# Chunked attention and a gated feed-forward network on one core: sums of the weights formed by GpSimd during the first pair, seven products one step earlier

## The chip, the core and the metric

The kernel runs on one core of a Trainium2 chip. The core has five engines that run side by side and wait for one another by semaphores: TensorE (PE, matrix products into PSUM), VectorE (DVE), ScalarE (ACT), GpSimd (POOL) and SyncE (SP, which here only issues DMAs). The metric is the device time of one execution in microseconds, lower is better; several executions are timed and the median is given.

## What is computed

Attention within chunks of 64 rows, for 8 batches, 8 heads, 576 rows and 64 columns a head; its output, heads side by side, is a matrix of 4608 rows and 512 columns, and goes through a gated network of width 1536:

```python
scores = scale * np.matmul(q_c, k_c.transpose(0, 1, 2, 4, 3))
attn = np.exp(scores - np.max(scores, axis=-1, keepdims=True))
attn = attn / (np.sum(attn, axis=-1, keepdims=True) + 1e-09)
out = np.matmul(attn, v_c)
...
g = x @ w_gate
silu = g * (1.0 / (1.0 + np.exp(-g)))
return (silu * (x @ w_val) @ w_out).astype(np.float32)
```

## The kernel before

**Rows and steps.** The 4608 rows are nine groups of 512 ("batches" a0, a1 and so on in the code; `N` is 512). The width of 1536 is cut into twelve *steps* of 128 (`NF` is 12). In a step f, the gate and the value of 128 columns are formed for a group (512 columns of moving data), multiplied after the Silu, and projected back to 512 columns, added up over the steps in PSUM. Every operand is a pair of a high and a low part, and every product takes three matmuls (low by high, high by low, high by high).

**Seven products instead of eight.** Two groups together can be treated as a 2 x 2 block product, by Winograd's form of Strassen's method: 7 products of half the depth instead of 8. It needs sums and differences of the blocks of x (`x1`, `x2`, `x4`, `x5` beside the plain blocks) and of the four quarters of a step's weights (`Quarters.sums`: three instructions, then a high part by a cast, `upper`, and a low part by a subtraction, `lower`). In matmuls of 512 columns a step of two groups has 48 products plainly and 42 with seven; the projection of one group adds 12.

**The stages.**
1. *Opening*, groups 0 and 1: their attention, then the steps 0 to 11 while the weights arrive in raw form and are split (`Up`, `Out`). Steps below `SEVEN` (6) are plain (the loop `for f in range(1, SEVEN)`, products at L494), the later ones use seven products (`first_seven`, products at L898). Only group 0 is projected here (L572 to L574); group 1's products are put off to DRAM. During steps 2 to 5, DVE and ACT form the sums of x (class `Raw`; L812, L815, L821, L825), and in every step those of the next step's weights (L157 to L159, L171, L174), which are saved to DRAM for the pairs (`kept_t`), as are the weights themselves (`save_w`, `kept_w`).
2. *Projection of group 1*, with the attention of group 2 beside it.
3. *The single batch*, group 2: twelve plain steps in the order 4 to 11, 0 to 3, the attention of groups 3 and 4 beside it. GpSimd forms sums of the output weights (class `WeightSums`, L1385 to L1394) and, at the fifth and sixth place, the weight sums of step 0 (`FirstQuarters`, L193).
4. *Three pairs*, groups 3 and 4, 5 and 6, 7 and 8: seven products a step (`both_steps`, `gated_pair`), with the left half of the projection; then the right half, itself by Strassen's method (`second_steps`, 30 *units* of a kind and a couple of steps, L560). Each step loads its weights and weight sums from DRAM (`load_weights`), two steps ahead, when the buffers are free. The attention of the next pair is spread over the places of the current one: dictionaries `middle`, `beside`, `behind` and `bursts` say what is added at which step, and where in it.

**Order of the work.** PE, ACT and DVE run their instructions in the order of the program text. SP does so in the opening alone; afterwards SP's and GpSimd's instructions are placed by a planner at the time at which it expects them ready, so a load may be issued long before its place in the text. All queues are in order once placed: an instruction that waits holds all those behind it.

**Buffers.** Tiles with the same tag share memory, and a tile waits for the release of its predecessor. The tags of the change: `w0` to `w11` (weights of the steps, reused; `moved(i)` is `w` of (i + 4) mod 12, so `moved(11)` is `w3`), `w8`, `w9`, `th`, `turned`, and the banks `ps_a`, `ps_gv`, `ps_o`. In `gated_pair`, ACT copies the first product out of its bank (L1173) before PE can go on with the third.

Of the kernel before, what the change touches and what calls it, by code (L numbers as in the profile page):

```python
# [8 lines left out]
F32 = mybir.dt.float32  # L9
F32R = mybir.dt.float32r  # L10
# [23 lines left out]
def attn_then_gated_ffn(ctx: ExitStack, tc: tile.TileContext, qk, v, wgv, wo, out):  # L34
# [147 lines left out]
    SEVEN, EARLY = 6, 4  # L182
# [4 lines left out]
    class FirstQuarters(Quarters):  # L187


        def again(self):  # L190
            self.both = const.tile([P, 2, 4 * Q], F32R, name="th", tag=moved(1))
            w, self.t = w_both[self.f].bitcast(F32), self.both[:, 0].bitcast(F32)
            nc.gpsimd.tensor_tensor(out=self.t, in0=w[:, 0], in1=w[:, 1], op=ALU.add)  # L193

        def sums(self):
            s = self.both[:, 1].bitcast(F32).rearrange("p (i q) -> p i q", q=Q)
            super().sums(self.t, s, nc.gpsimd)

        def place(self):
            return [self.both[:, 0], self.both[:, 1]]  # L200

# [589 lines left out]
    quarters = Quarters(1)  # L791
    quarters.sums(w.t)
# [4 lines left out]
    quarters.upper()  # L797
# [30 lines left out]
    SUM_AT = {1: (0, 0), 2: (0, 1), 4: (1, 0), 5: (1, 1)}  # L828
# [4 lines left out]
    def begin():  # L833
# [4 lines left out]
    ahead = {3: lambda: raw[0].upper(1, 0), 4: lambda: raw[0].upper(2, 1)}  # L838
    beside = {2: begin,
              3: lambda: (raw[0].whole(a0, 0, S2), raw[0].both(S4, S2, S4, ALU.subtract)),  # L840
              4: lambda: (raw[0].lower(2), raw[0].upper(4, 2)),
              5: lambda: (raw[0].whole(a0, 1, S5), raw[0].both(S5, S5, S2, ALU.subtract), raw[0].upper(5, 3))}
    within = {2: lambda: raw[0].both(S1, S1, S4, ALU.add),
              3: lambda: (raw[0].lower(1), raw[0].both(S2, S1, S2, ALU.subtract)),
              4: lambda: raw[0].lower(4), 5: lambda: raw[0].lower(5)}

    for f in range(1, SEVEN):
# [4 lines left out]
        if f > 2:  # L852
            quarters.save()
            if f <= EARLY:
                save_w(f - 1)
# [6 lines left out]
        if f <= 2:  # L862
            quarters.lower()
            quarters.save()
        quarters = Quarters(f + 1)
# [13 lines left out]
        quarters.sums(w.t)  # L879
# [4 lines left out]
        quarters.upper()  # L884
        down[f + 1].scale()
        if f > 1:
            quarters.lower()
# [691 lines left out]
```

## Time and profile before

| | us |
|---|---|
| median of 3 runs | 852.75 |
| lowest, highest | 852.13, 853.79 |
| the profiled execution | 852.76 |
| its span, first to last instruction | 851.0 |
| opening, steps from 1 on | about 42 to 181 |
| single batch | about 222 to 324 |
| first, second, third pair | from about 324, 502 and 682 |

The profile is of one execution. Its page gives the busy time of each engine, the chain of work that ended last, and groups of instructions with mean durations; other views show instructions in order of time, with the idle time before each and what ended it, or busy times by stretch. A line of the profile such as `L494` is a line of the code printed above. The granted clock of PE was at its full value throughout (the page's row of slices shows 9 in all forty). A matmul's shown duration overlaps the next one's, so PE's pace is read from the distance of starts. DMA moved 231 MB, 272 GB/s in the mean, and more than 300 in most of the first 325 us.

### The profile page before, as it was taken

What the parts mean: (1) busy time and instruction counts of PE and PEld (TensorE: products, weight loads), DVE (VectorE), ACT (ScalarE), POOL (GpSimd) and SP (SyncE); (2) the same over time, 40 slices, a digit from 0 to 9 for tenths busy, and PEclk for the clock granted to TensorE, in tenths of its full rate; (3) what the DMA queues carried; (4) which work ended last, traced back from release to release, by engine and by line L of the source; (5) the groups of instructions that cost most, each with busy time, mean ns of one, the idle gap of its engine ahead of it and who ended that gap; (6) DMA issues with size and microseconds to landing.
All of it is one profiled execution on the core that took longest, in us unless ns stands there. A gap on an engine that the chain in (4) does not pass through costs nothing.

```text
span 851.0 us, 16650 instructions
## 1 busy us (share of the span) xinstructions
PE 834.4 (98%) x6695; PEld 745.2 (88%) x6695; DVE 611.9 (72%) x958; ACT 433.5 (51%) x647; POOL 136.7 (16%) x101
## 2 busy tenths in 40 slices
PE   7999999999999999999999999999999999999997
PEld 6788888888888888888889998888889988888997
DVE  5889999964698865668886976688758944333475
ACT  5867788753525245535335744453337633333353
POOL 1300000000055451233110002313010002222100
PEclk9999999999999999999999999999999999999999
DMA  9697888799999899866669879666478576666643
GB/s 352 264 364 281 333 308 310 290 362 317 417 297 385 287 384 328 301 211 232 232 210 335 262 229 331 231 233 228 169 230 284 169 258 228 233 231 231 229 177 115
DMA packets 96653, 231.26 MB, mean 272 GB/s; under 512 B 32064, under 2 KB 58176, under 8 KB 83904
## 3 DMA queue, kind: packets, MB, share of 16 engines
q1 hardware_dynamic: 94848, 227.31, 74.5%
q10 hardware_dynamic: 1728, 2.88, 1.0%
q8 instruction: 53, 0.87, 0.4%
q14 instruction: 24, 0.20, 0.1%
HBM read 177.21 MB, written 52.95 MB: 270 GB/s over the span
## 4 chain that ended last, share of the span: by engine, by line
PE 78%; DVE 8%; DMA 6%; ACT 2%; issue 2%; SPq 1%; POOL 1%; DVEq 0%; ACTq 0%; POOLq 0%
PE ps_a L898 23%; PE ps_gv L898 17%; PE ps_o L560 14%; PE ps_gv L494 8%; PE ps_gv L560 6%; PE ps_o L572 3%; PE ps_o L573 3%; PE ps_o L574 3%; DMA v_t<-in_v 2%; PE ps_a L296 2%; DMA qk_t<-r 1%; DMA both<-o 1%; DVE h L544 1%; PE ps_a L384 1%; DVE w L139 1%
## 5 line engine op out<-in xcount | busy, mean ns | idle before, releaser
L898 PE MATMUL ps_a<-x,factors 128*128 128x512 f32 x864 | 210.7, 380 | 0.2 <-issue 0.2
L898 PEld LDWEIGHTS ps_a<-x,factors 128*128 128x128 f32 x864 | 154.3, 190 | 17.7 <-issue 0.7
L898 PE MATMUL ps_gv<-x,factors 128*128 128x512 f32 x648 | 157.5, 379 | 0.1
L898 PEld LDWEIGHTS ps_gv<-x,factors 128*128 128x128 f32 x648 | 122.4, 189 | 17.8 <-PE ps_a L898 0.4
L1220 POOL TENSOR_TENSOR kept<-kept 128x512 f32<-128x512 f32 x39 | 56.9, 1459 | 369.1 <-DVE kept L544 364.7
L494 PE MATMUL ps_gv<-xh,w 128*128 128x512 f32 x384 | 112.7, 379 | 0.0
L371 DVE STREAM_TRANSPOSE turned<-s_sb 32x256 f32<-32x256 f32 x192 | 83.7, 436 | 3.1
L494 PEld LDWEIGHTS ps_gv<-xh,w 128*128 128x128 f32 x384 | 72.4, 189 | 11.1 <-issue 0.8
L70 ACT CAST hh<-kept 128x512 fp32r<-128x512 f32 x111 | 67.2, 618 | 28.7 <-PE ps_o L560 15.4
L494 PE MATMUL ps_gv<-xl,w 128*128 128x512 f32 x192 | 71.8, 383 | 2.2 <-ACT s_sb L387 1.2
L902 DVE TENSOR_TENSOR kept<-kept,ps_gv 128x512 f32<-128x512 f32 x30 | 20.6, 688 | 67.2 <-PE ps_gv L898 67.0
L1194 ACT ACTIVATE kept<-ps_a 128x512 f32<-128x512 f32 x36 | 21.5, 598 | 89.7 <-PE ps_a L898 89.3
L71 DVE TENSOR_TENSOR hl<-kept,hh 128x512 fp32r<-128x512 f32 x84 | 57.3, 688 | 12.4 <-ACT hh L70 12.0
L544 DVE SCALAR_TENSOR_TENSOR kept<-v,kept 128x512 f32<-128x512 f32 x66 | 45.7, 693 | 24.2 <-ACT kept L1194 18.0
L560 PE MATMUL ps_o<-sums,hh 128*128 128x256 f32 x504 | 62.7, 275 | 0.0
L560 PEld LDWEIGHTS ps_o<-sums,hh 128*128 128x128 f32 x504 | 59.3, 192 | 0.4 <-DVE hh L71 0.4
L560 PEld LDWEIGHTS ps_o<-both,hh 128*128 128x128 f32 x288 | 51.4, 189 | 6.9
L572 PE MATMUL ps_o<-both,hl 128*128 128x512 f32 x144 | 55.3, 384 | 0.3 <-DMA both<-o 0.3
L573 PE MATMUL ps_o<-both,hh 128*128 128x512 f32 x144 | 54.6, 379 | 0.0
L574 PE MATMUL ps_o<-both,hh 128*128 128x512 f32 x144 | 54.6, 379 | 0.0
L560 PE MATMUL ps_o<-both,hh 128*128 128x256 f32 x288 | 53.5, 276 | 0.0
L902 DVE TENSOR_TENSOR v<-v,ps_a 128x512 f32<-128x512 f32 x42 | 28.9, 687 | 21.9 <-PE ps_a L898 19.3
(163 smaller groups left out, 1415.6 us busy)
## 6 DMA issues: line engine op xcount, KB each, us to landing
factors<-w SPq DMA_DIRECT2D x36, 1024.0 KB, 4.9
factors<-t SPq DMA_DIRECT2D x36, 1024.0 KB, 7.0
sums<-sums SPq DMA_DIRECT2D x36, 512.0 KB, 6.0
w<-w SPq DMA_DIRECT2D x16, 1024.0 KB, 8.8
t<-th SPq DMA_DIRECT2D x24, 512.0 KB, 4.5
raw<-in_wgv SPq DMA_DIRECT2D x11, 1024.0 KB, 8.5
both<-o SPq DMA_DIRECT2D x22, 512.0 KB, 8.7
qk_t<-in_qk SPq DMA_DIRECT2D x10, 1024.0 KB, 9.0
```

Source lines behind the costliest of these rows:

```text
L70: nc.scalar.copy(out=hi, in_=src)
L71: (engine or nc.vector).tensor_tensor(out=lo, in0=src, in1=hi.bitcast(F32), op=ALU.subtract)
L371: nc.vector.transpose(out=self.turned[to:to + 32, p:p + 2, j, :, 32 * (i % 2):32 * (i % 2) + 32], in_=src[32 * i:32 * i + 32, :, o // 2, 3 ...
L494: nc.tensor.matmul(ps, w, in_turn(x), start=first and (k, i) == which[0], stop=last and (k, i) == which[-1])
L544: nc.vector.scalar_tensor_tensor(out=h, in0=pv, scalar=2.0 ** -8, in1=h, op0=ALU.mult, op1=ALU.mult)
L560: nc.tensor.matmul(banks[t // 2][:, t % 2], h[u][:, t * P:(t + 1) * P], in_turn(w[v]), start=first and t % 2 == 0 and n == 0, stop=n == 2, ...
L572: nc.tensor.matmul(o, hl[:, ts], woh, start=f == a.steps[0], stop=False)
L573: nc.tensor.matmul(o, hh[:, ts], wol, start=False, stop=False)
L574: nc.tensor.matmul(o, hh[:, ts], woh, start=False, stop=f == a.steps[1])
L898: nc.tensor.matmul(ps, w[u][:, k], in_turn(x[i][v][:, k]), start=first and k == 0 and n == 0, stop=k == NK // 2 - 1 and n == 2, skip_group ...
L902: nc.vector.tensor_tensor(out=t, in0=t, in1=ps, op=ALU.add)
L1220: engine.tensor_tensor(out=out, in0=one, in1=two, op=op)
```

## The change

1. `SEVEN` goes from 6 to 5: step 5 of the opening uses seven products. The sums of x are therefore formed in steps 1 to 4 instead of 2 to 5, in the tiles `th` and `w9` instead of `w8` and `w9`, and the weights of steps 2 and 3 are saved one step earlier.
2. The opening forms weight sums only for step 5 on. Those of steps 0 to 4 are formed by GpSimd from the saved weights (`LateQuarters`): step 0's in the single batch one step later than before, those of 4, 1, 2 and 3 in the first pair, with a cast on ACT, and saved to DRAM.
3. The pairs take the steps in the order 8, 9, 10, 11, 6, 7, 4, 5, 0, 1, 2, 3 (`STEPS`), and the units follow it.
4. The loads of values for the next pair's second group are issued behind the load of the left half (`asked_left`) instead of behind that of the weights.
5. At the very end, the last sums are combined and written half by half.

```diff
-    SEVEN, EARLY = 6, 4
+    SEVEN, EARLY = 5, 4
...
-    class FirstQuarters(Quarters):
...
+    class LateQuarters(Quarters):
+        def begin(self, tag, halves=None):
+            self.both = const.tile([P, 2, 4 * Q], F32R, name="th", tag=tag)
+            both = self.both.bitcast(F32)
+            if halves is None:
+                halves = both
+                nc.sync.dma_start(out=both, in_=kept_w[self.f])
+            nc.gpsimd.tensor_tensor(out=both[:, 0], in0=halves[:, 0], in1=halves[:, 1], op=ALU.add)
+            self.sums(both[:, 0], both[:, 1].rearrange("p (i q) -> p i q", q=Q), nc.gpsimd)
...
+        def split(self):
+            self.upper()
+            self.lower(nc.gpsimd)
...
-            self.at = [const.tile([P, 2, NK // 2 * N], F32, name="sums", tag=tag) for tag in ("w8", "w9")]
+            self.at = [const.tile([P, 2, NK // 2 * N], F32, name="sums", tag=tag) for tag in ("th", "w9")]
...
+    ahead = {2: lambda: raw[0].upper(1, 0), 3: lambda: raw[0].upper(2, 1)}
+    beside = {1: begin,
+              2: lambda: (raw[0].whole(a0, 0, S2), raw[0].both(S4, S2, S4, ALU.subtract)),
+              3: lambda: (raw[0].lower(2), raw[0].upper(4, 2), raw[0].whole(a0, 1, S5)),
+              4: lambda: raw[0].upper(5, 3)}
+    within = {1: lambda: raw[0].both(S1, S1, S4, ALU.add),
+              2: lambda: (raw[0].lower(1), raw[0].both(S2, S1, S2, ALU.subtract)),
+              3: lambda: (raw[0].both(S5, S5, S2, ALU.subtract), raw[0].lower(4)), 4: lambda: raw[0].lower(5)}
...
-        if f > 2:
-            quarters.save()
-            if f <= EARLY:
-                save_w(f - 1)
+        if 1 < f < EARLY:
+            save_w(f)
...
-        if f <= 2:
-            quarters.lower()
-            quarters.save()
-        quarters = Quarters(f + 1)
...
-        quarters.sums(w.t)
+        if f + 1 == SEVEN:
+            quarters = Quarters(SEVEN)
+            quarters.sums(w.t)
...
-            asked[:] = [nc.sync.dma_start(out=t.bitcast(F32), in_=kept[f]).ins]
+            nc.sync.dma_start(out=t.bitcast(F32), in_=kept[f])
...
-        nc.sync.dma_start(out=both.bitcast(F32), in_=kept_o[f][:, :, :HALF])
+        asked_left[:] = [nc.sync.dma_start(out=both.bitcast(F32), in_=kept_o[f][:, :, :HALF]).ins]
...
+    COUPLES = 4, 5, 3, 2, 0, 1
+    STEPS = [2 * j + i for j in COUPLES for i in range(2)]
...
-            for h, w in last_two:
-                narrow(g, (2 * j, 2 * j + 1), h, w, False)
...
+            for ks in ((0,), (1,)) if pair.last else ((0, 1),):
+                for h, w in last_two:
+                    narrow(g, [2 * j + k for k in ks], h, w, False)
...
+                combine(here["u2"][j], g[j], ALU.add, ks)
+                put_out(pair, 0, 1, j, here["u2"][j], ks, (nc.sync, nc.scalar if pair.last else nc.sync))
...
+    late_sums = [LateQuarters(f) for f in (0, 4, 1, 2, 3)]
...
-        if i == 4:
-            q0.again()
-            q0.sums()
-        elif i == 5:
-            q0.upper()
-            q0.lower(nc.gpsimd)
-            q0.save()
+        if i == 5:
+            late_sums[0].begin("turned", w_both[0].bitcast(F32))
+        elif i == 6:
+            late_sums[0].split()
+            late_sums[0].save()
...
-            middle = {2: lambda: c.exponents(0, NP), 5: lambda: n.a[1].exponents(0, NP), 10: lambda: load_late(n.a[1], asked[0]), 11: lambda: (n.s1(), n.s4())}
+            middle = {2: lambda: c.exponents(0, NP), 5: lambda: n.a[1].exponents(0, NP), 10: lambda: load_late(n.a[1], asked_left[0]), 11: lambda: (n.s1(), n.s4())}
...
+            for q, tag, (f, beginning), (g, splitting), (k, saving) in zip(late_sums[1:], (moved(11), "turned", moved(11), moved(11)),
+                                                    ((0, middle), (1, middle), (3, behind), (5, middle)),
+                                                    ((0, behind), (2, middle), (4, behind), (6, behind)),
+                                                    ((1, middle), (2, behind), (5, middle), (7, middle))):
+                then(beginning, f, lambda q=q, tag=tag: q.begin(tag))
+                then(splitting, g, q.split)
+                then(saving, k, q.save)
```

More of the change, by code (lines that the diff above doesn't have):

```diff
@@ L883, in attn_then_gated_ffn @@
         h1 = gate(a1, f)
-        quarters.upper()
+        if f + 1 == SEVEN:
+            quarters.upper()
         down[f + 1].scale()
-        if f > 1:
+        if f + 1 == SEVEN:
             quarters.lower()
@@ L1165, in turn_of @@
                 turns([t])
+        factors = loaded[STEPS[i]]
         ps1 = ps_a.tile([P, N], F32, name="ps_a", tag="ps_a")
@@ L1184, in gated_pair @@
         turn_of(1)
[L1185 removed]
+        seventh(ps1, pair.x, factors, 4, False)
         add(v2, ps1)
[L1187 removed]
+        seventh(ps2, pair.x, factors, 5, False)
         add(v1, ps2)
         times(h, v1)
[L1190 removed]
+        if i == NF - 1:
             prepare_unit(pair, 0)
         turn_of(2)
[L1193 removed]
+        seventh(ps1, pair.x, factors, 6, False)
         nc.scalar.activation(h2, ps1, AF.Silu, scale=2.0 ** -8)
@@ L1196, in gated_pair @@
         turn_of(3)
-        return parts(pair, f, h)
+        return parts(pair, i, h)
     HALF = DM // 2
@@ L1223, in left_half @@
         both = wp.tile([P, 2, DM], F32R, name="both", tag="wo")[:, :, :HALF]
-        nc.sync.dma_start(out=both.bitcast(F32), in_=kept_o[f][:, :, :HALF])
+        asked_left[:] = [nc.sync.dma_start(out=both.bitcast(F32), in_=kept_o[f][:, :, :HALF]).ins]
         return both[:, 0], both[:, 1]
     def both_steps(pair, middle, beside, behind, bursts, nothing=lambda: None):
-        pair.kept, pair.factors = [], {}
+        pair.kept, pair.factors = {}, {}
         pair.banks = [[ps_o.tile([P, 2, HALF], F32, name="ps_o") for _ in range(2)] for _ in range(2)]
-        for f in range(NF):
-            if f % 2 == 0:
-                pair.kept.append(places(f // 2))
-            kept = pair.kept[-1]
+        for i, f in enumerate(STEPS):
+            if i % 2 == 0:
+                kept = pair.kept[f // 2] = places(i // 2)
             wo_f = left_half(f)
-            p = gated_pair(pair, f, kept[2 + f % 2], kept[f % 2], [0] if f in bursts else range(T),
-                           middle.get(f, nothing), beside.get(f, nothing))
-            if f in bursts:
+            p = gated_pair(pair, i, kept[2 + i % 2], kept[i % 2], [0] if i in bursts else range(T),
+                           middle.get(i, nothing), beside.get(i, nothing))
+            if i in bursts:
                 turns([1])
-                bursts[f]()
+                bursts[i]()
                 turns([2, 3])
-            behind.get(f, nothing)()
-            if f % 2 and f < NF - 1:
+            behind.get(i, nothing)()
+            if i % 2 and i < NF - 1:
                 sums_of_rows(kept)
             pending.append((p, wo_f))
-            if f + 2 < NF:
-                load_weights(f + 2)
-            elif f == NF - 2:
-                two_steps(pair, "T1", (0, 2), moved(7))
-                two_steps(pair, ("T1", "T2"), (4, 0), moved(8))
+            if i + 2 < NF:
+                load_weights(STEPS[i + 2])
+            elif i == NF - 2:
+                two_steps(pair, "T1", (4, 2), moved(7))
+                two_steps(pair, ("T1", "T2"), (0, 4), moved(8))
     WEIGHT_SUMS = {"T1": 0, "T3": 1, "T2": 2, "T4": 3}
@@ L1351, in second_steps @@
             if i in last_rows:
-                sums_of_rows(pair.kept[-1], [last_rows[i]], nc.vector)
+                sums_of_rows(pair.kept[COUPLES[-1]], [last_rows[i]], nc.vector)
             loads.get(i, nothing)()
```

75 lines of the change are left out of this document (25 added, 50 removed).

## The prediction

> **What bounds the kernel now.** I read the page's first part, then the chain that ended last, then busy times by stretch. The first two lines below are the page's; the others are stretches of the opening: four plain steps (from the first output matmul of one step to that of the next, steps 1-2, 2-3, 3-4, 4-5) and two seven-product steps. Columns: length, then busy us of PE, PEld, DVE, ACT and POOL, granted clock, DMA share, GB/s.
>
> ```profile
> PE 834.4 (98%) x6695; PEld 745.2 (88%) x6695; DVE 611.9 (72%) x958; ACT 433.5 (51%) x647; POOL 136.7 (16%) x101
> PE 78%; DVE 8%; DMA 6%; ACT 2%; issue 2%; SPq 1%; POOL 1%; DVEq 0%; ACTq 0%; POOLq 0%
> ...
> 47.61:60.56 12.95, 12.95 (x61) 11.34 (x60) 9.95 (x15) 8.62 (x11) 0.00 (x0) 1.00 1.02 385
> 60.56:74.02 13.46, 13.22 (x62) 11.26 (x60) 12.80 (x17) 10.23 (x12) 0.00 (x0) 1.00 0.58 225
> 74.02:88.20 14.18, 13.48 (x61) 11.18 (x60) 13.55 (x18) 9.85 (x13) 0.00 (x0) 1.00 0.96 369
> 88.20:101.16 12.96, 12.96 (x62) 11.34 (x61) 12.14 (x17) 9.22 (x12) 0.00 (x0) 1.00 0.91 349
> ...
> 108.92:121.21 12.29, 12.08 (x56) 9.96 (x54) 11.58 (x16) 10.11 (x14) 0.00 (x0) 1.00 0.75 282
> ...
> 133.48:145.53 12.05, 11.92 (x55) 10.13 (x54) 11.05 (x16) 10.32 (x14) 0.00 (x0) 1.00 0.72 262
> ```
>
> PE bounds nearly everything, so time comes only from fewer matmuls or from PE's gaps. The reader is to see that two of the four plain steps are longer than the others (13.46 and 14.18 against 12.95) while DVE fills 12.80 and 13.55 of them: there DVE sets the pace. The chain and PE's timeline say the same:
>
> ```profile
> 50.36 7.78 PE ps_gv L494 x36
> ...
> 68.36 1.05 ACT th L171
> ...
> 70.59 0.68 DVE h L544
> ...
> 71.32 0.48 PE L494 MATMUL ps_gv<-xl,w 128*128 128x512 f32 x1 [0.24 <-DVE h L544]
> ...
> 85.51 0.48 PE L494 MATMUL ps_gv<-xl,w 128*128 128x512 f32 x1 [0.51 <-DVE h L544]
> ```
>
> The first row gives the price of a matmul of 512 columns: 7.78 / 36 = 0.216 us. (The shown mean durations of about 380 ns overlap; 60 x 0.216 = 12.95 is the stall-free plain step.) The next two are the cause of the first gap: the cast of the weight sums (L171), DVE's lower half behind it, and only then the product h (L544) that frees the bank PE waits for.
>
> **Part 1, the opening.** Steps 1 to 4 lose their weight sums. What one set costs DVE, and one operation on the sums of x:
>
> ```profile
> L157 DVE TENSOR_TENSOR ts<-t 128x512 f32<-128x512 f32 x11 | 7.6, 689 | 0.2
> L158 DVE TENSOR_TENSOR ts<-t,ts 128x256 f32<-128x256 f32 x11 | 4.7, 425 | 0.4
> L174 DVE TENSOR_TENSOR th<-ts,th 128x1024 fp32r<-128x1024 f32 x11 | 13.4, 1221 | 2.2 <-ACT th L171 2.2
> L812 DVE TENSOR_TENSOR sums<-xh,xl 128x1024 f32<-128x1024 f32 x4 | 4.9, 1221 | 0.8 <-ACT t L96 0.8
> ...
> w<-w SPq DMA_DIRECT2D x16, 1024.0 KB, 8.8
> ```
>
> A set is 0.69 + 0.43 + 0.43 (L159 has L158's shape) + 1.22 = 2.77 us of DVE, 1.05 of ACT, and two saves of 512 KB on SP. The twelve operations on the sums of x (1.22 each) stay, one step earlier; at most four fall into a step, one more than in the fullest stretch now. So the fullest becomes at most 13.55 - 2.77 + 1.22 = 12.0 of DVE, under PE's 12.95. I take all of the excess as gone: 13.46 + 14.18 + 12.96 - 3 x 12.95 = **-1.75** (bounds -1.75 and 0, if another wait takes over).
>
> Step 5 goes from 48 + 12 matmuls to 42 + 12. A seven-product step is 12.05 long in the steady state and 12.29 at first, not 54 x 0.216 = 11.65, because ACT and DVE pace it. So 12.95 - 12.05 = **-0.90** (bounds -0.66 by the longer row and -1.30 by matmuls alone). The weights of steps 2 and 3 are saved one step earlier, ahead of the tiles that overwrite them; the save lands in 8.8, inside one step, so I cost it at nothing. The cover is that step of 12.95: a save that landed later would hold the cast into the tile on ACT, and its lateness would be PE's. SP has eight saves fewer before it.
>
> **Part 2, the single batch.** The sums of step 0 move from steps i = 4, 5 to i = 5, 6.
>
> ```profile
> 255.26 2.37 POOL L193 TENSOR_TENSOR th<-w 128x1024 f32<-128x1024 f32 x1 [2.43 <-PE ps_a L296]
> 255.81 2.36 DVE L312 TENSOR_TENSOR s_sb<-s_sb,top 128x512 f32<-128x512 f32 x1
> ...
> 264.87 2.04 ACT L387 COPY s_sb<-ps_a 128x512 f32<-128x512 f32 x4
> ...
> 266.46 0.38 PE L494 MATMUL ps_gv<-xl,w 128*128 128x512 f32 x1 [1.22 <-ACT s_sb L387]
> ...
> 384.24 0.69 DVE L312 TENSOR_TENSOR s_sb<-s_sb,top 128x512 f32<-128x512 f32 x1
> ```
>
> DVE's subtraction takes 2.36 where it takes 0.69 without GpSimd: it waits until GpSimd's 2.37 are over. Behind it come the exponents on ACT, then ACT's copies, then PE, idle 1.22. With GpSimd's addition a step later DVE is 1.67 earlier, more than the 1.22: **-1.2** (bounds -1.2 and 0; one step later DVE has mostly transposes, and its products have a step's slack).
>
> [...]
>
> **Part 3, the first pair.** Four sets of sums come in: per set a load and a save of 1 MB on SP, GpSimd's chain, one cast (1.05) on ACT. PE is never their direct user for many steps (the new order of steps puts 0 to 4 last), but ACT is in order, and behind its cast stands the copy that frees PE's bank.
>
> ```profile
> 315.97 5.18 PE ps_gv L494 x24
> ...
> 337.11 1.25 ACT L588 ACTIVATE o_sb<-ps_o 128x512 f32<-128x512 f32 x2 [0.65 <-PE ps_o L574]
> 339.06 0.59 ACT L1173 COPY kept<-ps_a 128x512 f32<-128x512 f32 x1 [0.70 <-PE ps_a L898]
> ...
> 340.48 1.25 PE L898 MATMUL ps_a<-x,factors 128*128 128x512 f32 x5
> ...
> L174 POOL TENSOR_TENSOR th<-th 128x1024 fp32r<-128x1024 f32 x1 | 2.4, 2383 | 0.0
> L157 POOL TENSOR_TENSOR th<-th 128x512 f32<-128x512 f32 x1 | 1.6, 1609 | 0.1
> L158 POOL TENSOR_TENSOR th<-th 128x256 f32<-128x256 f32 x1 | 0.7, 735 | 0.0
> ...
> factors<-t SPq DMA_DIRECT2D x2, 1024.0 KB, 12.3
> ...
> factors<-w SPq DMA_DIRECT2D x36, 1024.0 KB, 4.9
> ...
> 397.90 3.76 POOL L336 TENSOR_TENSOR s_sb<-s_sb,z 128x1024 f32<-128x1024 f32 x2
> ...
> 405.78 1.46 PE L898 MATMUL ps_a<-x,factors 128*128 128x512 f32 x6
> ```
>
> The cast of step 4's sums stands after the output copies (338.36) and before the copy at 339.06. With R the time at which GpSimd has the sums, the copy ends at R + 1.05 + 0.59, and PE wants it at 340.48: the stall is R - 338.84, and nothing up to there. R: the buffer is free when the products end at 321.15; the load takes 4.9 (mean of all) to 12.3 (those issued from 285 to 325, nearest in time); then 2.37 + 1.61 + 0.73 + 0.73 = 5.44. R lies between 331.5 and 338.9, later by what SP is behind. I take 0.8 (bounds 0 and 4). The same holds for step 3's cast behind i = 6: there PE wants the bank at 405.78, so the sums by 404.1, and GpSimd, if it scales the rows first (until 401.66), has them at 407.1, 3 late; if it takes the sums first, in time. I take 0.7 (bounds 0 and 3). For DVE blocked by GpSimd's longer operations I take 0.5 (bounds 0 and eight of them x 1.67 = 13; nearer to 0, DVE being idle for 28% of the span). Behind GpSimd's new operations stand the pair's sums of rows, wanted only much later; behind a load on SP that waits for its buffer stand the left halves and the next queries, and a load ahead of those is within the bound of 4. Sum **+2.0**.
>
> **Part 4, the second pair.** The values for the last product with the attention are now issued behind the load of the left half instead of behind the weights.
>
> ```profile
> 603.42 0.37 SPq L1224 DMA_DIRECT2D both<-o  x1
> ...
> 614.00 0.32 SPq L1158 DMA_DIRECT2D factors<-t  x1
> 614.37 0.43 SPq L276 DMA_DIRECT2D v_t<-in_v  x1
> ...
> 627.77 0.68 PE L384 MATMUL ps_a<-turned,v_t 64*64 64x64 f32 x28 [1.54 <-DMA v_t<-in_v]
> ```
>
> SP issued the left half at 603.42 and the values only behind the weights of 614.00, and PE waited 1.54 for the last of these loads. Issued some 10 us earlier they are there: **-1.5** (bounds -1.6 and 0).
>
> **Part 5, the end.** The last sums are combined and written half by half.
>
> ```profile
> 841.89 6.44 SPq L1285 DMA_DIRECT2D out<-o_sb  x9
> ...
> 846.63 0.76 DVE L1278 SCALAR_TENSOR_TENSOR o_sb<-ps_gv,o_sb 128x256 f32<-128x256 f32 x2 [0.58 <-PE ps_gv L560]
> ```
>
> One of the two combinations (0.38) leaves the tail, but SP issues its writes back to back, nine in 6.44 us, up to the end, so the last can move little: **-0.15** (bounds -0.4 and 0). The other order of steps and units has the same instructions, tiles and turns: nothing, hidden behind PE's 98%.
>
> **The sum.** -1.75 - 0.90 - 1.2 + 2.0 - 1.5 - 0.15 = -3.5. The profiled execution took 852.76 (span 851.0), the median of the runs is 852.75: **849.3 us**. Without part 3's cost it is 847.3; with its waits at their upper ends (4 + 3 + 1) 855.3.
>
> **The rivals.**
> *A, the stalls only change their cause* (0.10). DVE is relieved, but the next late thing, ACT or a raw load, holds PE in the opening; single batch and second pair keep their gaps. For it: ACT is busy 10.23 of 13.46; against: it has over 3 us to spare, and every gap named DVE. Left are -0.90 - 0.15 and about half of part 3: 852.7.
> *B, GpSimd's chain comes late and ACT waits* (0.08), the slower side. If GpSimd takes step 1's set first (its buffer is free earlier), R is 338.9 + 5.4 + its wait, 344 or more, and each us past 338.84 is a us of PE. With the gains of 5.5, it decides from R = 344.3, and by 0.2% from 346.0. At R = 349: 852.76 - 5.5 + 10.2 = 857.5. Against it: SP issues loads as soon as their buffers are free, well ahead of the step.
> *C, blocked DVE* (0.12). By the 255.81 row each of the eight long GpSimd operations can cost DVE 1.67; if two or three reach PE, part 3 is 1.5 + 4.2 and the time 853.0. [...]
> *The forecast* 0.70.
>
> **How the numbers follow.** The forecast's own range is 846.8 (nothing lost in the pair, a little more won) to 851.0. Rivals A and C reach 853.0, B lies outside: the range is 846.5 to 853.0. 0.2% (1.7 us) is about what a measurement of this kernel tells from no change. Faster by more: the forecast and a part of A and C, 0.78; within: the rest of A and C, 0.14; slower: B, 0.08.
>
> **What would show it.** Plain steps of 12.95 throughout, and a first seven-product step near 101; no PE gap at the single batch's fifth step and none before the second pair's last attention product; in the first pair ACT's wait for GpSimd at the cast (L171's successor) and PE's gap behind it, at the starts of its second and eighth step. The forecast is wrong if these gaps exceed 3 us, or if the opening's end does not come 2 us or more earlier.

## The result and the profile after

The changed kernel takes 862.88 us in the median of 4 runs (859.43 to 865.53), the kernel before 852.55 beside it (852.13 to 853.79): 1.0116 times as long, 95% interval 1.0076 to 1.0156. It is slower by 10 us where 3.5 us less were forecast, and it scatters more. The profiled execution took 861.71 (span 859.9) against 852.76 (span 851.0).

The span's 8.9 us are split by reading off when each stage's first matmul starts in the two traces:

| stage | before | after | difference | forecast |
|---|---|---|---|---|
| opening, to its last seven-product matmul | 180.39 | 177.38 | -3.0 | -2.65 |
| projection of group 1 | 41.36 | 41.03 | -0.3 | 0 |
| single batch | 101.83 | 100.03 | -1.8 | -1.2 |
| first pair, left half | 136.71 | 152.32 | **+15.6** | +2.0 |
| second pair, left half | 137.45 | 134.97 | -2.5 | -1.5 |
| third pair, left half | 122.97 | 123.22 | +0.2 | 0 |
| the end, from the last product of the third pair | 46.63 | 47.32 | +0.7 | -0.15 |

The right halves of the first two pairs are equal. So every gain that was forecast came, the end went the wrong way by little, and the first pair lost eight times what it was given. First the opening, busy times by stretch (columns as in the prediction), three plain steps of the kernel after, from output matmul to output matmul:

```profile
47.23:60.19 12.96, 12.96 (x62) 11.34 (x61) 9.98 (x13) 8.69 (x11) 0.00 (x0) 1.00 0.96 319
60.19:73.15 12.96, 12.96 (x62) 11.35 (x61) 10.97 (x14) 8.63 (x11) 0.00 (x0) 1.00 0.59 239
73.15:86.11 12.96, 12.96 (x62) 11.35 (x61) 8.76 (x12) 8.60 (x11) 0.00 (x0) 1.00 0.83 287
```

Each is 12.96 long and PE is busy for all of it; DVE's 13.55 of before is 10.97 at most. Now the first pair of the kernel after, PE's timeline, those rows alone that begin with idle time (in brackets, with what ended it):

```profile
334.24 1.53 PE L896 MATMUL ps_gv<-x,factors 128*128 128x512 f32 x6 [0.35 <-PE ps_a L896]
348.54 0.38 PE L564 MATMUL ps_o<-both,hl 128*128 128x256 f32 x1 [2.14 <-DVE hl L71]
359.03 1.56 PE L896 MATMUL ps_gv<-x,factors 128*128 128x512 f32 x6 [1.34 <-DMA factors<-t]
385.95 0.38 PE L564 MATMUL ps_o<-both,hl 128*128 128x256 f32 x1 [1.67 <-DVE hl L71]
388.09 2.83 PE L896 MATMUL ps_a<-x,factors 128*128 128x512 f32 x6 [1.76 <-ACT kept L1172]
412.46 0.38 PE L564 MATMUL ps_o<-both,hl 128*128 128x256 f32 x1 [1.59 <-DVE hl L71]
414.61 2.06 PE L896 MATMUL ps_a<-x,factors 128*128 128x512 f32 x6 [1.77 <-ACT kept L1172]
```

The brackets add up to 10.6. A matmul is shown 0.38 long and the next one starts after 0.216 (0.28 and 0.112 at 256 columns), so a shown end lies some 0.16 behind the earliest next start, and from start to start the seven gaps are 12.0. Most of the rest begins in the fifth and the last row: six matmuls take 2.83 and 2.06 instead of 1.56. Start to start they are 0.427 apart there instead of 0.216, for 3.4 us each time: 1.8 and 1.7 us more. The stretches say why (the third number from the end is the granted clock, which was at half for 3.41 us in each):

```profile
375.00:400.00 25.00, 21.56 (x102) 18.43 (x101) 20.52 (x25) 11.84 (x15) 9.80 (x6) 0.93 0.67 242
400.00:425.00 25.00, 21.64 (x103) 18.59 (x102) 20.71 (x33) 7.37 (x12) 14.96 (x10) 0.93 0.65 248
```

The clock was 1.00 in all other stretches of 25 us up to 850. All these gaps but the one for factors share one cause, seen in the timelines of GpSimd, DVE and ACT around the fourth and fifth row (DVE's first two lines are the same meeting in the first step):

```profile
380.17 2.36 POOL L196 TENSOR_TENSOR th<-th 128x1024 f32<-128x1024 f32 x1 [6.96 <-DMA th<-w]
382.61 1.61 POOL L157 TENSOR_TENSOR th<-th 128x512 f32<-128x512 f32 x1
384.29 1.05 POOL L158 TENSOR_TENSOR th<-th 128x256 f32<-128x256 f32 x1
385.42 1.05 POOL L159 TENSOR_TENSOR th<-th 128x256 f32<-128x256 f32 x1
```

```profile
327.92 3.74 DVE L548 SCALAR_TENSOR_TENSOR kept<-v,kept 128x512 f32<-128x512 f32 x2
333.44 0.69 DVE L316 TENSOR_TENSOR s_sb<-ps_a,top 128x512 f32<-128x512 f32 x1
...
380.39 4.37 DVE L548 SCALAR_TENSOR_TENSOR kept<-v,kept 128x512 f32<-128x512 f32 x2
384.69 1.21 DVE L71 TENSOR_TENSOR hl<-kept,hh 128x512 fp32r<-128x512 f32 x1
```

```profile
386.51 1.04 ACT L171 CAST th<-th 128x1024 fp32r<-128x1024 f32 x1 [2.77 <-POOL th L159]
387.46 0.58 ACT L1172 COPY kept<-ps_a 128x512 f32<-128x512 f32 x1
```

GpSimd begins at 380.17, when its load has landed, and 0.2 us later DVE comes to the step's two products (L548 is L544 of before, 0.69 each): they take 4.37, until both long GpSimd operations are over, and the low part `hl`, 0.69 before, takes 1.21. PE waits for `hl` at 385.95. ACT stands 2.77 at the cast of the same sums, and behind the cast stands the copy that frees PE's bank: 388.09. The small gap of the first row, 334.24, belongs to DVE as well: the profile names PE itself, but PE goes on 0.11 after DVE's operation of 333.44 has ended, which stood behind the 3.74, and 0.10 after the same operation in the three other traces that have this gap.

### The profile page after: what moved, and what is told of

The parts are those of the page before. It is cut to its first block, busy times and chain, and to the rows that moved or that the text cites. A ratio compares the mean times of both kernels' runs of the same rounds, so it can differ in the third digit from the quotient of the medians.

```text
span 859.9 us, 16648 instructions
## 1 busy us (share of the span) xinstructions
PE 836.2 (97%) x6689; PEld 745.7 (87%) x6689; DVE 614.3 (71%) x945; ACT 434.4 (51%) x650; POOL 167.4 (19%) x121
## 4 chain that ended last, share of the span: by engine, by line
PE 80%; DVE 7%; DMA 5%; POOL 3%; ACT 3%; issue 2%; SPq 0%; ACTq 0%; POOLq 0%; DVEq 0%
PE ps_a L896 21%; PE ps_gv L896 15%; PE ps_o L564 13%; PE ps_gv L498 12%; PE ps_gv L564 5%; PE ps_o L576 3%; PE ps_o L578 3%; PE ps_o L577 3%; DMA th<-w 2%; PE ps_a L300 2%; DMA v_t<-in_v 2%; PE ps_a L388 1%; DMA factors<-t 1%; DVE h L548 1%; DVE w L139 1%
## 5 line engine op out<-in xcount | busy, mean ns | idle before, releaser
L896 PE MATMUL ps_gv<-x,factors 128*128 128x512 f32 x648 | 159.5, 383 | 1.8 <-DMA factors<-t 1.3
L498 PE MATMUL ps_gv<-xh,w 128*128 128x512 f32 x352 | 103.2, 380 | 0.0
L498 PEld LDWEIGHTS ps_gv<-xh,w 128*128 128x128 f32 x352 | 66.4, 189 | 9.5 <-ACT xh L653 0.2
L548 DVE SCALAR_TENSOR_TENSOR kept<-v,kept 128x512 f32<-128x512 f32 x66 | 56.5, 861 | 23.2 <-ACT kept L1193 16.3
L900 DVE TENSOR_TENSOR kept<-kept,ps_gv 128x512 f32<-128x512 f32 x30 | 20.6, 687 | 67.8 <-PE ps_gv L896 67.6
L71 DVE TENSOR_TENSOR hl<-kept,hh 128x512 fp32r<-128x512 f32 x84 | 59.9, 718 | 12.5 <-ACT hh L70 12.0
L498 PE MATMUL ps_gv<-xl,w 128*128 128x512 f32 x176 | 65.4, 382 | 0.0
L1386 POOL TENSOR_TENSOR qk_t<-qk_t 128x512 f32<-128x512 f32 x6 | 10.9, 1822 | 230.5 <-DMA qk_t<-r 230.5
```

Of the source, the lines that this page charges most:

```text
L71: (engine or nc.vector).tensor_tensor(out=lo, in0=src, in1=hi.bitcast(F32), op=ALU.subtract)
L498: nc.tensor.matmul(ps, w, in_turn(x), start=first and (k, i) == which[0], stop=last and (k, i) == which[-1])
L548: nc.vector.scalar_tensor_tensor(out=h, in0=pv, scalar=2.0 ** -8, in1=h, op0=ALU.mult, op1=ALU.mult)
L896: nc.tensor.matmul(ps, w[u][:, k], in_turn(x[i][v][:, k]), start=first and k == 0 and n == 0, stop=k == NK // 2 - 1 and n == 2, skip_group ...
```

## The experiments

Times of each kernel stand beside runs of the kernel before on the same chip (medians 851.82, 853.21, 852.79, 852.41 and 852.59 in five groups). The better measure of a part is the first pair's left half in the profile, 136.71 before and 152.32 after; it is given as "pair".

**Without GpSimd's operations.** In `LateQuarters`, for steps 1 to 4 (step 0's set in the single batch is formed as before):

```diff
                 nc.sync.dma_start(out=both, in_=kept_w[self.f])
+                self.s = both[:, 1]
+                return
             nc.gpsimd.tensor_tensor(out=both[:, 0], in0=halves[:, 0], in1=halves[:, 1], op=ALU.add)
             self.sums(both[:, 0], ..., nc.gpsimd)
...
-            self.lower(nc.gpsimd)
+            if self.f == 0:
+                self.lower(nc.gpsimd)
```

> Leaves out, in the first pair, GpSimd's five operations on each of the four late sets (the sum of the two parts, the three sums, the low part); their loads, their casts on ACT and their saves stay, so the sums of steps 1 to 4 are not formed. Theory (GpSimd is the cause: it blocks DVE's two-input products and the low parts, and holds ACT at the casts): of the 15.6 us that the first pair lost, only what the transfers cost stays, the 1.34 in front of its fourth step and a little beside it. Time 849, at most 851; granted clock 1.00. Rival (the transfers, 8 MB more in the pair, are the cause): the gaps stay, now in front of matmuls that wait for factors, and the time is 858 or more.

851.35 us (850.21 to 854.71), ratio 0.9994 (0.9977 to 1.0011); pair 143.12. So in the profiled execution 9.2 of the 15.6 go with GpSimd's work, less than the 14 expected, and 6.4 stay without it. PE's timeline of this kernel has two waits in the pair, both for loads, and the clock is at half from 356.30 on for 6.8:

```profile
355.14 1.83 PE L899 MATMUL ps_a<-x,factors 128*128 128x512 f32 x6 [2.03 <-DMA factors<-w]
358.27 2.93 PE L899 MATMUL ps_gv<-x,factors 128*128 128x512 f32 x6 [1.31 <-DMA factors<-t]
```

Theory and rival both had a part of it: GpSimd's work made most of the loss, and the transfers cost more than 1.34 as soon as PE, without the other waits, comes to them earlier.

**One cast later.** The cast of step 2's sums moves behind the copies of the next step:

```diff
-  ((0, behind), (2, middle), (4, behind), (6, behind)),
+  ((0, behind), (2, middle), (5, middle), (6, behind)),
```

> The cast of step 2's sums is moved on ACT from the end of the pair's fifth step to the middle of its sixth, behind the copies that free PE's banks. Theory (ACT in order: the copy L1172 stands behind a cast that waits for GpSimd): the gap of 2.03 us at 388.09 goes, and with it the half clock behind it (1.8 us); the gap in front of the projection at 385.95 (1.84), which DVE's late low part makes, stays, and so does all of the place two steps later. Time 859.1, 3.8 below the changed kernel. Rival (DVE's block alone makes the step late, and the copy would be late anyway): within 1 us of the changed kernel.

862.41 us (862.1 to 863.38), 1.0114 (1.0088 to 1.0141); pair 152.02: no gain. The gap at 388.09 and its half clock went, as the theory said. But the buffer was freed later, so step 3's load was issued at 401.07 instead of 396.00, GpSimd had its sums at 413.8, and the wait behind that cast grew from 1.77:

```profile
415.30 2.93 PE L896 MATMUL ps_a<-x,factors 128*128 128x512 f32 x6 [5.63 <-ACT kept L1172]
```

The mechanism is shown, the sum was wrong: the sets of steps 2 and 3 run through one buffer, and the wait taken out at the one returned at the other.

**The gaps filled.** Idle places of the sixth and eighth step are given matmuls without use:

```diff
+        def fill(n):
+            if pair.a[0].b == 3 and i in (5, 7):
+                for _ in range(n):
+                    nc.tensor.matmul(ps3, ..., start=True, stop=True, skip_group_check=True)
...
+        fill(8)
         turn_of(0)
+        fill(8)
         seventh(ps1, pair.x, factors, 2, False)
```

> The changed kernel with sixteen matmuls more in the sixth and in the eighth step of the first pair, eight ahead of the first projection and eight ahead of the third product, into a bank that the fourth product clears: they do no work and stand where PE is idle for 1.6 to 2.0 us. Theory (the granted clock halves because PE is idle for 3.5 of some 4 us): the clock stays 1.00, the 1.8 and 1.5 us of half speed go, and 32 matmuls cost nothing or some tenths: time 859.5, with the scatter of the runs under 2 us. Rival (the clock falls for a reason that lies outside of the gaps, so that more matmuls make it no better): 863 or more, clock 0.99 as before.

871.35 us (869.29 to 872.33), 1.0214 (1.0184 to 1.0244), worse than either theory said; pair 151.19. In the pair half of the theory holds: ACT still stands 2.79 at the cast of the sixth step, and the clock stays at 1.00. But the pair is only 1.1 shorter: the 32 matmuls are themselves 32 x 0.216 = 6.9 of PE where the four gaps were 7.7, and other waits appeared. And in the second pair, whose work is unchanged, PE stood twice in the middle of a product without any wait that the profile shows, and the clock was halved behind both. Stretches, then PE's timeline:

```profile
375.00:400.00 25.00, 24.36 (x123) 21.05 (x122) 21.34 (x25) 12.44 (x16) 10.80 (x6) 1.00 0.77 276
400.00:425.00 25.00, 24.14 (x124) 21.35 (x123) 22.25 (x36) 7.64 (x13) 15.60 (x12) 1.00 0.63 245
550.00:575.00 25.00, 22.93 (x226) 19.95 (x225) 13.91 (x24) 7.32 (x13) 7.95 (x5) 0.93 0.55 182
```

```profile
561.68 0.38 PE L896 MATMUL ps_a<-x,factors 128*128 128x512 f32 x1 [1.98 <-issue]
561.89 2.58 PE L896 MATMUL ps_gv<-x,factors 128*128 128x512 f32 x6
```

The trace has a lead. In this kernel each stall without a visible wait (one in the first pair, two in the second) has a packet of the instruction queue beside it (16 KB; the DMA view's q8, 53 packets in the whole run): it is over at 460.46, 560.25 and 643.03, and PE goes on at 461.66, 561.68 and 644.52, 1.2 to 1.5 later each time. So PE may have waited for its instructions; no run tests this, and why they came late stays open.

**The end as before.**

```diff
-            for ks in ((0,), (1,)) if pair.last else ((0, 1),):
+            for ks in ((0, 1),):
```

> The changed kernel with the end as it was before: the last sums are combined for both halves at once. Theory (PE's second half of a bank waits for DVE's combination of the first half, two gaps of 0.78 and 0.90 us): 0.7 to 1.5 us below the changed kernel, last matmul 1.6 earlier against the last unit. By the prediction it would be 0.15 above it.

861.02 us (859.36 to 861.84), 1.009 (1.0057 to 1.0124). From the last product of the third pair to the span's end it is 46.35, against 47.32 split and 46.63 before. Split, PE waits for DVE between the halves, twice (timeline of the kernel after):

```profile
853.47 0.49 PE L564 MATMUL ps_gv<-sums,hh 128*128 128x256 f32 x2 [0.64 <-DVE o_sb L1276]
855.60 0.49 PE L564 MATMUL ps_gv<-sums,hh 128*128 128x256 f32 x2 [0.52 <-DVE o_sb L1276]
```

Both halves are columns of one tile, and PE went on to the second 0.06 after DVE had combined the first (at 853.41 and 855.54).

**GpSimd in pieces.** The same work in operations of 128x256:

```diff
+            for i in range(4):
+                q = slice(i * Q, (i + 1) * Q)
+                nc.gpsimd.tensor_tensor(out=both[:, 0, q], in0=halves[:, 0, q], in1=halves[:, 1, q], op=ALU.add)
```

> GpSimd's operations on the late sets are cut into pieces of 128x256 (four for the sum of the parts, four for the low part, two for the first of the sums): the same work and the same transfers. Theory (a DVE operation with two inputs from SBUF waits for the one GpSimd operation that runs, and gets its turn behind it): each wait falls from up to 2.37 us to about 0.6, the late low parts' gaps in front of the projection (2.30, 1.84 and 1.75 us at 348.54, 385.95 and 412.46) fall to under 1 us together; the waits of ACT's casts for GpSimd (2.03 twice) stay, and the half clock behind them (1.8 and 1.5), which needs both gaps, goes. Time 862.9 - 5 - 3.3 = 854.6. Rival (GpSimd's back-to-back operations hold DVE for the whole chain, so that the pieces change nothing): 862 to 864, or more by the pieces' fixed cost.

866.25 us (863.92 to 867.86), 1.0147 (1.0122 to 1.0173); pair 154.86. The theory's mechanism came true and its time did not. DVE at the place where after's L548 pair took 3.74, GpSimd beside it, and PE:

```profile
327.85 2.36 DVE L556 SCALAR_TENSOR_TENSOR kept<-v,kept 128x512 f32<-128x512 f32 x2
330.13 1.22 DVE L71 TENSOR_TENSOR hl<-kept,hh 128x512 fp32r<-128x512 f32 x1
```

```profile
326.41 3.24 POOL L204 TENSOR_TENSOR th<-th 128x256 f32<-128x256 f32 x4 [7.16 <-DMA th<-w]
```

```profile
358.16 1.88 PE L904 MATMUL ps_gv<-x,factors 128*128 128x512 f32 x6 [3.54 <-DMA factors<-t]
389.88 2.85 PE L904 MATMUL ps_a<-x,factors 128*128 128x512 f32 x6 [4.71 <-ACT kept L1180]
417.08 2.75 PE L904 MATMUL ps_a<-x,factors 128*128 128x512 f32 x6 [4.29 <-ACT kept L1180]
```

DVE's products take 2.36 instead of 3.74, and no gap in front of the projection is left. But GpSimd is slower: four pieces take 2.77 even where DVE leaves them alone (the low part at 416.62), and 3.24 beside DVE, for what took 2.37. So its sums come later, and ACT stands longer at the casts. PE, no longer held in front of the projection, also comes earlier to the factors of the fourth step, and waits 3.54 for them instead of 1.34. The wait has moved from DVE's path to ACT's and to the loads.

**The values later.** 

```diff
-  6: lambda: (more(10), load_values(c)),
+  6: lambda: (more(10), load_late(c, asked_left[0])),
```

> The loads of values for the next pair's first group, at the end of the seventh step in the text, are issued behind the load of that step's left half, as part 4 does for the second group; in the changed kernel and in the one before SyncE issues them some five steps earlier, at 339 to 348, ahead of the factors of the fourth step. Theory (these factors come late because SyncE is held by loads that wait for their buffers and by the saves, and because they share the DMA engines with the rest): the gap of 1.51 us at 359.03 goes, in the run without GpSimd's work the two of 2.19 and 1.73 in its place; time 861.4. Rival (the saves of the sums, which wait for GpSimd, hold SyncE): the gap stays, and the time is within 0.5 us of the changed kernel's.

860.96 us (858.8 to 861.47), 1.0081 (1.0054 to 1.0108); pair 151.86. The gap stays (1.51 at 358.69, ended by the load of the factors). SyncE's waits show why. In the changed kernel the loads of values did hold it (5.4 in two waits, for writes out of their buffers), and it issued these factors at 348.35 and 349.67. With those loads moved, the query load into `w3` holds it instead, 8.2 until the set in `w3` has been saved, and the factors go out at 347.17 and 348.30, 1.2 and 1.4 earlier; the last of them lands only some 0.3 earlier (PE goes on at 358.69 instead of 359.03). One holder stood behind the other.

**One buffer changed.** Step 4's set is formed in `th`:

```diff
-  (moved(11), "turned", moved(11), moved(11)),
+  ("th", "turned", moved(11), moved(11)),
```

> The changed kernel with one buffer changed: the sums of step 4, the first of the late sets, are formed in the memory of the tag th, which is idle until the fourth step, and not in that of w3, in which the queries of the next pair's second group are awaited; these queries stand on SyncE ahead of the factors of the fourth step. Theory (SyncE holds the factors until the set is saved out of w3): the gap of 1.51 us at 359.03 goes, the gaps that GpSimd makes stay, time 861.4. Rival (the factors are late because the DMA engines are shared with the sets): the gap stays, 862.9.

863.1 us (862.01 to 865.94), 1.0118 (1.0086 to 1.0149); pair 156.15. The gap before the fourth step is gone, but that does not show the theory: the factors went out no earlier (349.62 and 350.41, the values' loads ahead of them as before), and PE came to them later, at 362.25 instead of 359.03. For the load into `th` was there later: GpSimd began at 334.37 instead of 327.06, and now the second step pays, half clock included:

```profile
341.28 2.92 PE L896 MATMUL ps_a<-x,factors 128*128 128x512 f32 x6 [5.11 <-ACT kept L1172]
```

**Step 4's sums back in the opening, three late sets.** Together with pieces, values later, the last cast later and the whole end (only the first of these edits is shown):

```diff
-        if f + 1 == SEVEN:
-            quarters = Quarters(SEVEN)
+        if f + 2 >= SEVEN:
+            quarters = Quarters(f + 1)
...
-    late_sums = [LateQuarters(f) for f in (0, 4, 1, 2, 3)]
+    late_sums = [LateQuarters(f) for f in (0, 1, 2, 3)]
```

> The changed kernel with the end as it was before, GpSimd in pieces, the values behind the left half, and the sums of step 4 formed in the opening again, by DVE, where the fourth plain step has 8.8 us of DVE in 13.0; the sums of steps 1, 2 and 3 take the places that those of 4, 1 and 2 had, and the last cast stands in the middle of the sixth step, behind the copies. Theory: the opening keeps its 3.0 us, the single batch its 1.8 and the second pair its 2.5, and of the first pair's 15.6 less than 2 stay: 846 to 848, below both kernels. Rival (the fourth plain step becomes DVE's again, or late sums cost the pair what they cost before): 850 or more.

851.68 us (850.43 to 852.78), 0.9981 (0.9969 to 0.9993); pair 141.50. The opening keeps 2.9 of its 3.0. The pair's 4.8 were in five waits, the largest again for factors (1.47 at 359.43). SyncE's timeline names the holder: the query load into w3, which waited 8.7 for the set to be saved, and the factors right behind it:

```profile
348.88 0.38 SPq L280 DMA_DIRECT2D qk_t<-in_qk  x1
349.36 0.42 SPq L1166 DMA_DIRECT2D factors<-w  x1
349.87 0.38 SPq L1166 DMA_DIRECT2D factors<-t  x1
```

**DVE forms the sums.** As the last kernel, but `begin` only loads, the first set is in `th`, away from the queries, and of the pair's late sets GpSimd keeps nothing but the low part of step 3, in pieces. DVE's work and ACT's casts stand at given places of the first six steps:

```diff
+  (middle, 0, lambda: q1.begin("th")), (behind, 0, q1.form_loaded), (middle, 1, q1.upper), (beside, 1, q1.lower),
+  (middle, 1, lambda: q2.begin("turned")), (middle, 2, q2.form_loaded), (beside, 2, q2.upper), (behind, 2, q2.lower),
+  (behind, 3, lambda: q3.begin(moved(11))), (behind, 4, q3.form_loaded), (beside, 5, q3.upper), (behind, 5, q3.pieces),
```

> As best1, but the late sums of steps 1, 2 and 3 are formed by DVE (sum of the parts, three sums, low part of steps 1 and 2), at places of the first six steps where DVE has 4 us or more to spare, and GpSimd keeps only the low part of step 3, in four pieces; step 1's set is in the memory of th, step 2's in that of turned, step 3's in that of w3; the casts stand on ACT behind the copies. Theory (what the pair lost was GpSimd's block of DVE, ACT's waits for GpSimd, and SyncE's wait for w3): of the 4.8 us that the first pair of best1 still loses at most 1 stays, the 0.28 in the single batch goes: 846 to 848. Rival (with DVE's 12 us more in the first six steps, DVE itself becomes late): 850 or more, with gaps that end at DVE's low part or its additions.

852.71 us (850.93 to 854.93), 0.9995 (0.9978 to 1.0013); pair 141.70. The waits for GpSimd and for loads are gone (the fourth step's factors go out at 342.05 and 343.68 instead of 349.36 and 349.87); in their place are three waits for DVE, whose additions were queued behind the new work:

```profile
354.09 1.56 PE L911 MATMUL ps_a<-x,factors 128*128 128x512 f32 x6 [1.34 <-DVE v L915]
390.71 1.56 PE L911 MATMUL ps_a<-x,factors 128*128 128x512 f32 x6 [2.50 <-DVE v L915]
402.06 1.56 PE L911 MATMUL ps_a<-x,factors 128*128 128x512 f32 x6 [0.68 <-DVE v L915]
```

**The same work at idle places of DVE.** Two of the sets change buffers with it, the queries go to `turned`, and step 3's set is loaded behind the left half:

```diff
+  (middle, 0, lambda: q1.begin(moved(11))), (middle, 0, lambda: q2.begin("th")),
+  (behind, 0, q1.form_loaded), (middle, 1, q1.upper), (middle, 1, q2.form_parts),
+  (beside, 1, q1.lower), (behind, 1, q1.save),
+  (middle, 2, q2.form_sums), (beside, 2, q2.upper), (behind, 2, q2.lower), (behind, 2, q2.save),
+  (middle, 3, later_load), (behind, 3, q3.form_loaded), (beside, 4, q3.upper),
+  (beside, 4, q3.pieces), (middle, 5, q3.save)
...
-  bursts = {..., 3: lambda: scores(n.second()), ...}
+  bursts = {..., 3: lambda: scores(n.second(), at="turned"), ...}
```

> As best2, with DVE's work on the late sets put where best2's profile shows DVE idle: step 1's set is formed at the end of the first step (memory of w3), step 2's in the middle of the second and third (memory of th), step 3's at the end of the fourth (w3 again), so that nothing is added to the sixth step; the queries of the next pair's second group are awaited in the memory of turned instead of w3, and step 3's set is loaded behind the left half of the fourth step. Theory (best2's 5.0 us of gaps at 354.09, 390.71 and 402.06 come from where DVE's work stood, not from its amount): at most 1 us of them stays; time 847.5 to 849 where best2 has 851. Rival (any 4 us a set more of DVE, or the transfers, cost the pair about what they cost now): 851 or more.

**848.11 us** (847.24 to 849.97) beside 852.41 of the kernel before: 0.9952, interval 0.994 to 0.9964, faster than both kernels. Pair 137.92, 1.2 over the kernel before; one wait of more than half a microsecond is left in it:

```profile
388.21 1.56 PE L917 MATMUL ps_a<-x,factors 128*128 128x512 f32 x6 [0.51 <-DVE v L921]
```

**And the same with GpSimd.** The sets' sums and low parts, and nothing else (the low part of step 3, GpSimd's already, is no longer in pieces):

```diff
-            self.form(self.loaded, self.loaded, nc.vector)
+            self.form(self.loaded, self.loaded, nc.gpsimd)
...
-  (beside, 1, q1.lower), ... (behind, 2, q2.lower), ... (beside, 4, q3.pieces)
+  (beside, 1, lambda: q1.lower(nc.gpsimd)), ... (behind, 2, lambda: q2.lower(nc.gpsimd)), ... (beside, 4, lambda: q3.lower(nc.gpsimd))
```

> As best3, with one thing changed: GpSimd, not DVE, does the sum of the parts, the three sums and the low part of the late sets of steps 1, 2 and 3, at the same places of the text, whole and not in pieces; loads, casts, saves and buffers are those of best3. Theory (the engine that forms the sums is the main cause of what the first pair lost: GpSimd's chain of about 6 us a set blocks DVE's operations with two inputs from SBUF, and its lateness holds the casts on ACT): gaps in front of the projection and of the third product come back in the first five steps, 4 to 9 us together, a part of it at half clock: 852 to 857. Rival (place, buffers and the order of the loads were the cause, and the engine matters little): 848 to 850.

853.44 us (851.78 to 855.37), 1.0006 (0.9993 to 1.0019), 5.3 over the kernel with DVE; pair 144.59. Two GpSimd operations in a row each hold one DVE operation, and the second of these is the low part that PE waits for. GpSimd, DVE and PE:

```profile
357.63 2.37 POOL L174 TENSOR_TENSOR th<-th 128x1024 fp32r<-128x1024 f32 x1 [4.89 <-ACT th L171]
359.96 2.78 POOL L201 TENSOR_TENSOR th<-th 128x1024 f32<-128x1024 f32 x1
```

```profile
358.07 2.47 DVE L567 SCALAR_TENSOR_TENSOR kept<-v,kept 128x512 f32<-128x512 f32 x1 [0.73 <-ACT kept L1214]
360.46 2.82 DVE L71 TENSOR_TENSOR hl<-kept,hh 128x512 fp32r<-128x512 f32 x1
```

```profile
363.34 0.58 PE L583 MATMUL ps_o<-both,hl 128*128 128x256 f32 x1 [3.53 <-DVE hl L71]
```

Behind that one gap the clock is halved again (0.86 in the stretch from 350 to 375). Buffers, loads and places in the text being equal, the engine is the cause of these 5 us.

**Part 4 alone, on the kernel before.**

```diff
-            asked[:] = [nc.sync.dma_start(out=t.bitcast(F32), in_=kept[f]).ins]
+            nc.sync.dma_start(out=t.bitcast(F32), in_=kept[f])
...
-        nc.sync.dma_start(out=both.bitcast(F32), in_=kept_o[f][:, :, :HALF])
+        asked[:] = [nc.sync.dma_start(out=both.bitcast(F32), in_=kept_o[f][:, :, :HALF]).ins]
```

> The kernel before with part 4 of the change alone: the values for the next pair's second group are issued behind the load of the left half instead of behind that of the weights. Theory (the prediction's: PE's wait for these values in the second pair goes, and what the changed kernel's second pair is shorter by, 2.5 us, is this alone): the second pair is 2.0 to 2.5 shorter, the rest stays: about 2.2 below the kernel before. Rival (a part of the 2.5 comes from the other order of steps): 1.5 or less.

852.27 us (850.33 to 854.35) beside 852.59, 0.9988 (0.9967 to 1.0009): not to be told from no change in time. In the profile the second pair's left half is 135.99, 1.46 shorter, and the wait of 1.54 for the values is gone. But the single batch, whose work is the same, is 1.0 longer: its two waits of 1.41 and 0.41 from start to start became 1.85 and 0.85. The other 1.0 of the changed kernel's 2.5 is for the most part a stall of PE without a visible wait, from start to start 0.41 at 606.56 before, 0.90 at 607.23 here, and none in the changed kernel.

## Why the prediction was wrong

The forecast was 849.3 in a range of 846.5 to 853.0, faster with 0.78. Point by point, by its own steps:

- *Part 1, -1.75 and -0.90*: right. All plain steps are 12.96, and the opening's end comes 3.0 earlier.
- *Part 2, -1.2*: right, -1.8. The gap at the fifth step is gone, 1.41 from start to start, and a later one of 0.41 for a load with it, which was not forecast.
- *Part 4, -1.5*: right in mechanism and size (1.46 alone). That the second pair gained 2.5 is luck: most of the other 1.0 is a stall without a visible wait, which this part does not explain.
- *Part 5, -0.15*: wrong sign, +0.7. SyncE's writes were priced, and not that both halves are in one tile and PE's second half waits for DVE's first (0.64 and 0.52).
- *Part 3, +2.0 with bounds 0 to 4, 0 to 3 and 0 to 13*: this is the step that failed, 15.6. Its three sums, and what was not in it:

*Step 4's cast, 0.8*: measured 0. GpSimd began at 327.06 and its sums were there at 333.4, inside the bounds, and no gap stands behind this cast (the 0.52 at 334.24 is DVE's); rival B, tied to this place, did not come about here. *Step 3's cast, 0.7*: measured 2.03. GpSimd did scale the rows first, which the text had as the bad one of two orders and weighed too low. *Step 2's cast* was not priced at all, and cost another 2.03: its load was issued at 373.53 and GpSimd began at 380.17, so the sums came 2.77 after ACT was at the cast. Rival B's mechanism was real, at two other casts, one of them never examined.

*Blocked DVE, 0.5*: measured 6.4 (0.52, 2.30, 1.84 and 1.75 from start to start). This is the largest error. The reason given, that DVE is idle for 28% of the span, was the error. What counts is not how idle DVE is but where GpSimd's chain falls: in the pair of the changed kernel all twelve of DVE's products and low parts (L548 and L71, both inputs in SBUF) that began while a GpSimd operation on the sets ran ended 0.54 or 0.55 after that operation, 1.02 to 2.90 long instead of 0.69, while an addition with one input in PSUM (L900, at 327.13) took its 0.69 beside the first of them. The two products and the low part follow each other on the path to PE, so one chain hits several of them. That is rival C, priced at 4.2 for two or three meetings; the bound of 13 was the right order of size. The pieces agree: quarter operations cut DVE's block from 3.74 to 2.36 for two products, and lengthened GpSimd's sum from 2.37 to 3.24, of which 0.4 is the pieces' own cost.

*Transfers, at most "within the bound of 4"*: 1.5 as it stood, 6.4 in the kernel without GpSimd's work, half clock included. The prediction named left halves and queries behind a waiting load, and not the factors, which stand behind the values and the queries; the gap went when neither was ahead of them any more and they went out 7 us earlier (the first kernel with DVE's sums).

*Half clock, not in the sum*: 3.5. The prediction took the full clock for granted. With the gaps filled it stayed full in the pair. So gaps cost more than their length, by some 30% here, and the runs' scatter seems to go with it: the four runs had mean clocks of 0.992 to 0.997, the two shorter ones the two higher. Together these terms are 15.5 of the 15.6.

Its signs of being right came true in the opening, the single batch and the second pair: 12.96 throughout, both gaps gone. Its sign of being wrong, gaps over 3 us behind the casts at the second and the eighth step, did not: they were 0 and 2.03. The loss lay in the steps between and in front of the projections, which the text did not price. What was promised beyond part 3 was there to be had: with three late sets instead of four, their sums on DVE and the end as before, the kernel is 4.3 us below the kernel before. Of that version's own cost, the pair still pays 1.2 and the fourth plain step, which forms step 4's sums again, 0.5.

## What to carry to other kernels

Work that was given to an idle engine was not free here: beside GpSimd's operations DVE's took up to 2.90 instead of 0.69. Ask which DVE operations GpSimd's chain will meet, not how idle DVE is on the average, and price the whole run of dependent operations that one chain can hit. Waits in the engines' queues moved here rather than went: the later cast and the pieces each removed the gap they aimed at and found it again further on (5.63 instead of 1.77 behind step 3's cast, 3.54 instead of 1.34 for the factors), and the values' loads made room for the next holder. When a gap is gone, look whether its load came earlier or the waiting engine later: with the other buffer it was the latter. Read the place for added work from the idle rows of the engine's own timeline; the same amount of work, moved by it (with some buffers and a load), made 852.7 into 848.1.

## What the hardware showed that was not expected

The granted clock fell to half for 3.41 us at a time (6.8 in the kernel without GpSimd's work); matmuls were then 0.427 apart instead of 0.216, and the two falls of the changed kernel cost 1.8 and 1.7 us. They came after gaps of 1.84 and 2.03, and of 1.75 and 2.03, from start to start. The length of a single gap does not decide: the clock fell after a gap of 2.14 (561.68 in the filled kernel), and not after one of 2.67 (390.71 in the kernel with DVE's sums, whose clock is 1.00 in the stretch from 375 to 400). A reading that fits these is idle time within a fixed raster. In the trace of the changed kernel the changes of the clock lie whole multiples of 3.41 apart, at 388.23, 391.64, 415.53 and 418.95, and once more at 859.27, behind the last matmul:

```profile
384.82:388.22 3.40, 0.51 (x2) 0.32 (x3) 3.33 (x5) 1.71 (x3) 2.17 (x3) 1.00 0.82 328
388.23:391.64 3.41, 3.41 (x9) 2.66 (x10) 3.35 (x4) 0.97 (x3) 1.75 (x1) 0.50 0.65 268
```

Adding up PE's idle time from start to start in each piece of that raster, the two falls in the course of this kernel follow pieces with 3.17 and 2.49 us. The longest wait of the kernel before from 30 us on, the 1.54 in front of 627.77 (1.70 from start to start), lies in one piece, counted back from the change of its clock at 850.53, and no fall follows it. The gap of 2.67 fits if it lay across a border. This is read off traces; no run was made to test it.

With thirty-two matmuls added in the first pair, PE had stalls of 1.4 to 2.6 us in both pairs, with no wait that the profile shows. The same kind of stall, 0.4 to 0.9 us, is at 606 in the kernel before and with part 4 alone, again 1.4 and 1.5 behind the end of an instruction packet, and absent in the changed kernel, so that differences of this size between two programs need not come from their work.
